# Reordering the end of an attention and soft-MoE kernel: last attention tiles, filler matmuls, weight pieces and output groups

## The chip, the cores and the metric

The kernel runs on one core of one Trainium2 chip. The time is device microseconds for one execution, from the program's start to its end. Inputs and outputs lie in HBM in float32; the matrix work is done in bf16 with float32 sums. PE is the matrix engine, ACT and DVE the two engines that read its results out of PSUM, POOL the engine that issues the loads (they cast to bf16 on the way), SP the one that issues the stores.

## The reference

Pooled attention for 8 batches and 8 heads (576 queries, 64 columns per head; keys and values are averaged over 8 positions to 72), and then a soft mixture of experts on its output:

```
x = softmax(q @ mean8(k).T / 8) @ mean8(v)          # 4608 x 512
logits = x @ phi                                    # 4608 x 32 slots
slot_input = softmax(logits, over the rows).T @ x   # 32 x 512
h = relu(slot_input[e] @ w1[e]); slot_out[e] = h @ w2[e]   # 8 experts, 4 slots each, 512 -> 1024 -> 512
out = softmax(logits, over the slots) @ slot_out    # 4608 x 512
```

`w1` and `w2` are 16.8 MB each in float32, q, k and v 9.4 MB each, the output 9.4 MB.

## The kernel before, in words

**Attention.** The batches go in four pairs, each in two halves of the heads (`qd`). Per step, `score_unit` makes one unit of scores and its exponential on ACT, and `u_tile` makes one of nine tiles of the attention output: PE writes it to PSUM, DVE takes a reciprocal (line 325) and scales the tile into `xsa` (line 331); with `by_scalar` ACT does the scaling in four pieces (line 329). `u_tile` of half `qd` runs for tiles 0 to 3 in the same half and for tiles 4 to 8 in the next one. Tiles 4 to 8 of the very last half are made after the loop, with DVE and ACT in turn.

**Dispatch.** For each pair the logits (`lg`) are summed over the heads, exponentiated on ACT into `ee`, and used as weights to sum the rows of x into 32 slots: nine matmuls into `G_ps` (line 346). Pairs 0 to 2 do this inside the next pair's loop, with the logits summed on PE. For the last pair (`by_vector`) DVE sums the logits of all nine tiles in one instruction (line 338). `turn` transposes `ee` into `cT`.

**Experts.** `hidden` (64 matmuls, line 521) and `turn_hidden` give `hT`. `second_layer` sums into `so_ps` over all experts, 8 groups of rows of w2 for each (line 542). w2 lands in buffers that the attention gives up: experts 0 to 3 in `big`, 4 and 5 in `qTa`, 6 and 7 in `xsa`. The last rows, listed in `PIECES`, come as left and right halves of the 512 columns, first all left halves, then all right ones (line 492); the rows of expert 7 may only be loaded when the last dispatch has read that part of `xsa`.

**Output.** `begin(half)` scales `so_ps` into `so_a` and, with the very last row group of w2 carried separately through `z_ps`/`zT`, makes the first output tiles; `product` multiplies by a tile of `cT` (line 600), `put` scales it by the row's reciprocal sum (`recR`, from `row_sums`) on ACT (line 573) or DVE (line 575). 36 tiles of 128 rows are stored in `GROUPS`; the first tiles are made and stored in halves of the columns, the others whole, one store per group. `busy` issues float32 matmuls into an unused buffer `idle`.

**Order.** Loads are issued by POOL in program order, on one queue; stores by SP in program order. A scheduling layer orders the other engines up to the end of attention; from there on every engine runs in the order written.

Of the kernel before, what the change touches and what calls it, by code (L numbers as in the profile page):

```python
# [18 lines left out]
def kernel(  # L19
# [10 lines left out]
    nc = tc.nc  # L30
# [26 lines left out]
    for rows in (2, 2, 2, 4, 6, 8, 12):  # L57
        GROUPS.append((rows, base))
        base += 128 * rows
# [29 lines left out]
    CUT6 = FJ - 5  # L89
# [13 lines left out]
    UNEVEN = 2560  # L103

    def load_w1(e, n, uneven=False):
        dst = w1_sb[:, e:e + n].rearrange("p e j f -> p e (j f)")
        src = moe_w1[e:e + n].rearrange("e (p j) f -> p e (j f)", j=DJ)
# [85 lines left out]
    nc.vector.memset(hz, 0.0)  # L193
# [12 lines left out]
    def after_k(p):  # L206
        if p + 1 < NP:
            q_sb[p + 1] = load(q, p + 1)
        if p == 1:
            load_w1(0, 1, True)  # L210
# [100 lines left out]
    def u_tile(pair, qd, t, ex, by_scalar=False):  # L311

        ps = ps_u.tile([128, HQ, XW + 1], FP, name="u_ps", tag="u")
# [20 lines left out]
    def dispatch(x, ps, ee, by_vector=False):  # L334

        if by_vector:
            lg = small.tile([128, 9, NS], FP, name="lg", bufs=1)
            nc.vector.reduce_sum(out=lg, in_=x[:, :, :, D:XW].rearrange("p t h c -> p t c h"), axis=AX.X)  # L338
        else:
            lg = ps_m.tile([128, 9, NS], FP, name="lg_ps", tag="m")  # L340
            for h in range(H):
                nc.tensor.matmul(out=lg, lhsT=ident, rhs=x[:, :, h, D:XW], start=(h == 0), stop=(h == H - 1))
        nc.scalar.activation(out=ee, in_=lg.rearrange("p t s -> p t () s").to_broadcast([128, 9, NG, NS]), func=AF.Exp)  # L343
        yield
        for t in range(9):
# [25 lines left out]
    def combine(pair):  # L371
# [3 lines left out]
        parts = dispatch(xs[pair], ps, ee)  # L375
        next(parts)
        yield
        next(parts, None)
# [8 lines left out]
    for g, (rows, base) in enumerate(GROUPS):  # L387
        cols = cT[:, :, base // 2:base // 2 + 64 * rows].rearrange("p r (i s) -> p s r i", s=rows // 2)
        n0 = sum(r for r, _ in GROUPS[:g])
# [3 lines left out]
    if GROUPS[0][0] == GROUPS[1][0] == 2:  # L393
        rest = rest[2:]
        quads.append((0, cT[:, :, 0:256].rearrange("p r (g i) -> p g r i", g=2)))
# [3 lines left out]
    for c, (n, t) in enumerate(quads + rest):  # L399
        for i in range(2 * t.shape[1]):  # L400
            place[n + i] = (i, c)

    def row_sums():
# [6 lines left out]
        sums = consts.tile([NC, 4, 128], FP)  # L410
        nc.scalar.copy(out=sums, in_=ps)
        ps = ps_m.tile([128, 4, NC], FP, name="RT_ps", tag="m")
# [25 lines left out]
    for pair in range(NP):  # L438
        for qd in range(2):
# [5 lines left out]
            for i in range(9):  # L445
# [5 lines left out]
                else:  # L451
                    u_tile(pair, qd, i - 5, ex)
# [96 lines left out]
    turn_hidden(1)  # L549
    nc.vector.reduce_sum(out=recC, in_=C, axis=AX.X)  # L550
# [8 lines left out]
    z_ps = ps_f.tile([128, 2, 128], FP, name="z_ps", tag="f")  # L559
    nc.tensor.matmul(out=z_ps, lhsT=hz, rhs=cT[:, :, 0:128], start=True, stop=True)  # L560
    zT = post.tile([128, 2, 128], BF)
# [6 lines left out]
    def busy(n):  # L568
        nc.tensor.matmul(out=idle[:, 0:n], lhsT=cTf[:, 0:128], rhs=cTf[:, 0:n], start=True, stop=True)

# [8 lines left out]

    out_a = exf.rearrange("p (n c) -> p n c", c=DM)  # L580
# [112 lines left out]
```

## Time and profile before

| | |
|---|---|
| time, median of 3 runs | 176.11 us (175.51 to 181.43) |
| span of the profiled execution | 179.6 us |
| PE, DVE, ACT busy | 129.9, 97.1, 88.3 us |
| loads' queue: share of the span of the 16 DMA engines | 83.9%, 30.48 MB |
| stores' queue (and one load) | 15.0%, 10.49 MB |
| read from and written to HBM | 61.93 MB, 9.44 MB |

The page gives no other time for the profiled execution than its span. A span lies inside its execution's time, so a span of 179.6 us doesn't fit the runs at 175.51 and 176.11 us; among the three it fits only 181.43 us, which would leave 1.9 us around the span. Times of the trace are counted from the span's start.

### The profile page before, as it was taken

How to read it: one execution, taken by the hardware profiler on the slowest of the kernel's cores; microseconds unless marked ns; L12 is line 12 of the kernel's file. 1: busy time of each engine (PE TensorE's matmuls, PEld its weight loads, DVE VectorE, ACT ScalarE, POOL GpSimd, SP SyncE). 2: the span in 40 equal slices, each digit the busy share in tenths (PEclk: the TensorE clock that was granted, in tenths of full speed). 3: DMA queues.
4: the chain of work that ended last, by engine and by line, in shares of the span. 5: the costliest groups of instructions: out<-in, count | busy, mean ns of one | idle time of the engine just before them, and what ended most of it. 6: DMA issues, size and time to landing. Idle time of an engine off the chain costs nothing.

```text
span 179.6 us, 2853 instructions
## 1 busy us (share of the span) xinstructions
PE 129.9 (72%) x1106; PEld 70.2 (39%) x1106; DVE 97.1 (54%) x258; ACT 88.3 (49%) x168; POOL 19.9 (11%) x37
## 2 busy tenths in 40 slices
PE   0006888999899999999998996512996988798000
PEld 0002463565555655556555543300443232333000
DVE  5403353387868588785888629764335000599200
ACT  3201238986887649876599726232012012799100
POOL 7000111052100040000100004000700300000000
PEclk9999999999999999999999669655559999999755
DMA  5999999999999999999999999999999990699995
GB/s 197 242 209 233 207 220 216 213 224 203 204 220 216 216 207 220 225 204 219 208 230 204 221 217 210 228 206 223 214 210 207 196 181 7 225 342 428 480 394 235
DMA packets 10780, 41.13 MB, mean 229 GB/s; under 512 B 768, under 2 KB 6656, under 8 KB 7184
## 3 DMA queue, kind: packets, MB, share of 16 engines
q0 software_dynamic: 7440, 30.48, 83.9%
q1 hardware_dynamic: 3328, 10.49, 15.0%
q8 instruction: 8, 0.13, 0.3%
q14 instruction: 4, 0.03, 0.0%
HBM read 61.93 MB, written 9.44 MB: 397 GB/s over the span
## 4 chain that ended last, share of the span: by engine, by line
PE 51%; ACT 17%; DVE 14%; DMA 6%; issue 3%; POOL 1%; DVEq 0%; ACTq 0%; POOLq 0%
PE pool_ps L234 9%; ACT exa L308 7%; DMA phi_f<-in_moe_phi_dram 6%; PE G_ps L346 6%; PE sc L306 6%; PE u_ps L320 6%; PE q_ps L266 5%; DVE w_sb L575 4%; PE h_ps L521 3%; DVE xsa L331 3%; PE so_ps L542 3%; ACT vmeans L240 2%; DVE lg L338 2%; PE R_ps L407 2%; PE turn_ps L250 2%
## 5 line engine op out<-in xcount | busy, mean ns | idle before, releaser
L308 ACT ACTIVATE exa<-sc 72x576 bf16<-72x576 f32 x64 | 39.5, 652 | 5.1 <-PE sc L306 4.3
L331 DVE TENSOR_TENSOR xsa<-u_ps,rec 128x384 bf16<-128x384 f32 x69 | 37.4, 554 | 1.3
L320 PE MATMUL u_ps<-vp,exa 72*128 72x97 bf16 (+1 forms) x320 | 27.3, 217 | 4.5 <-DVE xsa L331 3.7
L320 PEld LDWEIGHTS <-exa 72*128 72x128 bf16 (+1 forms) x320 | 18.2, 104 | 16.0 <-DVE xsa L331 6.8
L306 PE MATMUL sc<-qTa,kp 64*72 64x288 bf16 x128 | 22.0, 309 | 1.9 <-ACT exa L308 1.5
L234 PE MATMUL pool_ps<-big,pmat 128*128 128x512 bf16 x64 | 18.6, 411 | 0.7 <-ACT qTa L270 0.6
L325 DVE RECIPROCAL rec<-u_ps 128x4 f32<-128x4 f32 x72 | 11.5, 172 | 12.8 <-PE u_ps L320 12.6
L346 PE MATMUL G_ps<-xsa,ee 128*128 128x512 bf16 x36 | 12.0, 496 | 6.6 <-ACT ee L343 6.6
L266 PE MATMUL q_ps<-ident,big 128*128 128x128 bf16 x144 | 12.5, 231 | 0.2
L186 PE MATMUL phi_ps<-spread,sel 128*128 128x256 bf16 x4 | 1.3, 397 | 15.1 <-DVE spread L181 15.1
L600 PE MATMUL f_ps<-so,cT 128*128 128x512 bf16 (+1 forms) x42 | 10.2, 337 | 1.8 <-ACT w_sb L573 0.8
L306 PEld LDWEIGHTS <-kp 64*72 64x72 bf16 x128 | 8.0, 108 | 8.3 <-issue 3.1
L575 DVE TENSOR_SCALAR w_sb<-f_ps,recR 128x512 f32<-128x512 f32 (+1 forms) x17 | 10.5, 683 | 0.4 <-PE f_ps L600 0.2
L266 PEld LDWEIGHTS <-big 128*128 128x128 bf16 x144 | 9.6, 104 | 2.4 <-issue 0.7
L242 DVE TENSOR_REDUCE rsum<-rest_ps 128x64 f32<-128x512 f32 x8 | 5.5, 692 | 9.3 <-PE rest_ps L238 9.2
L270 ACT COPY qTa<-q_ps 128x768 bf16<-128x768 bf16 x8 | 6.3, 794 | 7.8 <-PE q_ps L266 7.8
L272 DVE COPY qTa<-q_ps 128x768 bf16<-128x768 bf16 x16 | 8.8, 553 | 2.1 <-PE q_ps L266 2.0
L573 ACT ACTIVATE w_sb<-f_ps,recR 128x512 f32<-128x512 f32 (+1 forms) x17 | 9.6, 638 | 0.5 <-PE f_ps L600 0.3
L492 POOL DMA_DIRECT2D xsa<-in_moe_w_dram x8 | 6.0, 754 | 26.2 <-PE G_ps L346 15.3
L346 PEld LDWEIGHTS <-ee 128*128 128x128 bf16 x36 | 4.1, 120 | 12.3 <-ACT ee L343 6.8
L234 PEld LDWEIGHTS <-pmat 128*128 128x128 bf16 x64 | 5.8, 103 | 6.4 <-issue 2.3
L240 ACT CAST vmeans<-pool_ps 128x1024 bf16<-128x1024 f32 x4 | 4.0, 1012 | 6.8 <-PE pool_ps L234 6.8
(104 smaller groups left out, 155.1 us busy)
## 6 DMA issues: line engine op xcount, KB each, us to landing
w_sb<-in_moe_w_dram POOLq DMA_DIRECT2D x2, 3072.0 KB, 37.2
big<-in_q_dram POOLq DMA_DIRECT2D x4, 1152.0 KB, 12.0
big<-in_v_dram POOLq DMA_DIRECT2D x4, 1152.0 KB, 15.8
big<-in_moe_w_dram POOLq DMA_DIRECT2D x1, 4096.0 KB, 40.0
big<-in_k_dram POOLq DMA_DIRECT2D x3, 1152.0 KB, 21.4
out_dram<-w_sb SPq DMA_DIRECT2D x1, 3072.0 KB, 10.8
qTa<-in_moe_w_dram POOLq DMA_DIRECT2D x1, 2048.0 KB, 30.4
out_dram<-w_sb SPq DMA_DIRECT2D x1, 2048.0 KB, 7.5
```

What stands on the lines that cost most here:

```text
L234: nc.tensor.matmul(out=ps, lhsT=pmat, rhs=src[:, t:full * POOL:POOL, :], start=(t == 0), stop=(t == POOL - 1))
L266: nc.tensor.transpose(out=ps[:, t].rearrange("p n i -> p (n i)"), in_=q_sb[pair][:, tt:tt + 2, :].rearrange("p t d -> p (t d)"), identity= ...
L272: nc.vector.tensor_copy(out=dst, in_=ps)
L306: nc.tensor.matmul(out=ps[:, r, 0:S // 2], lhsT=kp[pair][rows, n], rhs=qT[pair][rows, n].rearrange("p t i -> p (t i)"), start=True, stop=True)
L308: nc.scalar.activation(out=dst.rearrange("p r (i t) -> p r i t", t=NU), in_=ps[:, :, 0:S // 2].rearrange("p r (t i) -> p r i t", i=NI), fu ...
L320: nc.tensor.matmul(out=ps[rows, hh], lhsT=ex[b][:, hh].rearrange("p r t -> p (r t)")[:, c:c + rows.stop - rows.start], rhs=vp[(2 * pair + ...
L325: nc.vector.reciprocal(out=rec, in_=ps[:, :, XW])
L331: nc.vector.tensor_tensor(out=dst, in0=ps[:, :, 0:XW], in1=rec.rearrange("p h -> p h ()").to_broadcast([128, HQ, XW]), op=ALU.mult)
L346: nc.tensor.matmul(out=ps, lhsT=ee[:, t].rearrange("p g s -> p (g s)"), rhs=x[:, t, :, 0:D], start=(t == 0), stop=(t == 8))
L573: nc.scalar.activation(out=dst, in_=src, func=AF.Copy, scale=by)
L575: nc.vector.tensor_scalar(out=dst, in0=src, scalar1=by, scalar2=None, op0=ALU.mult)
L600: nc.tensor.matmul(out=ps, lhsT=tokens(n), rhs=so[:, cols], start=True, stop=True)
```

## The change

- Of the nine tiles of the last half, ACT scales tiles 1, 3, 5 and 7 (before: 4, 6 and 8); tiles 6, 7 and 8 are written to the score buffers (`spare`), which are free by then.
- The last pair's logits are summed on PE in three parts (`weigh`: tiles 0 to 3, 4 to 6, 7 and 8), each with its own exponential, and summed into `G_ps` part by part (`gather`).
- `row_sums` is split; its ten matmuls stand ahead of `z_ps` now, and its transposes (`turn_sums`) ahead of the second layer.
- The two pairs of 512-column float32 fillers give way to 24 and 40 bf16 fillers of 128 columns (`tiny`); six of 256 columns stand between the right halves.
- Five row groups of expert 6 are loaded whole instead of three, so 11 row groups come in halves instead of 13.
- Four tiles instead of two carry the last row group (`CARRY`), eight tiles instead of ten are made by halves, and groups are 2, 2, 2, 2, 4, 10, 14 rows instead of 2, 2, 2, 4, 6, 8, 12. The right halves are made two and two.
- The first expert's w1 is loaded in one transfer instead of four of unequal shape; one clearing of `hz` goes from DVE to POOL.

```diff
-    for rows in (2, 2, 2, 4, 6, 8, 12):
+    for rows in (2, 2, 2, 2, 4, 10, 14):
...
-    CUT6 = FJ - 5
+    CUT6 = 5
...
-    def load_w1(e, n, uneven=False):
...
-        if uneven:
-            for p0, p1 in ((0, 112), (112, 120), (120, 128)):
-                nc.gpsimd.dma_start(out=dst[p0:p1, :, 0:UNEVEN], in_=src[p0:p1, :, 0:UNEVEN])
-            dst, src = dst[:, :, UNEVEN:], src[:, :, UNEVEN:]
-        nc.gpsimd.dma_start(out=dst, in_=src)
+    def load_w1(e, n):
+        nc.gpsimd.dma_start(out=w1_sb[:, e:e + n].rearrange("p e j f -> p e (j f)"),
+                            in_=moe_w1[e:e + n].rearrange("e (p j) f -> p e (j f)", j=DJ))
...
+    def weigh(x, ee, t0, t1):
+        lg = ps_m.tile([128, t1 - t0, NS], FP, name="lg_ps", tag="m")
+        for h in range(H):
+            nc.tensor.matmul(out=lg, lhsT=ident, rhs=x[:, t0:t1, h, D:XW], start=(h == 0), stop=(h == H - 1))
+        nc.scalar.activation(out=ee[:, t0:t1], in_=lg.rearrange("p t s -> p t () s").to_broadcast([128, t1 - t0, NG, NS]),
+                             func=AF.Exp)
+    def gather(x, ps, ee, t0, t1):
+        for t in range(t0, t1):
             nc.tensor.matmul(out=ps, lhsT=ee[:, t].rearrange("p g s -> p (g s)"), rhs=x[:, t, :, 0:D],
...
-                    u_tile(pair, qd, i - 5, ex)
+                    u_tile(pair, qd, i - 5, ex, by_scalar=pair == NP - 1 and qd == 1 and i in (6, 8))
...
-    u_tile(*last[:2], 4, last[2], by_scalar=True)
-    for i in range(1, 5):
-        u_tile(*last[:2], 4 + i, last[2], by_scalar=i % 2 == 0)
-    for _ in dispatch(xs[NP - 1], G_ps, ee, True):
-        pass
+    for i in range(5):
+        u_tile(*last[:2], 4 + i, last[2], by_scalar=i % 2 == 1, ps=spare[i - 2] if i >= 2 else None)
+        if i == 2:
+            weigh(x, ee, 0, 4)
+    gather(x, G_ps, ee, 0, 4)
+    weigh(x, ee, 4, 7)
+    gather(x, G_ps, ee, 4, 7)
+    weigh(x, ee, 7, 9)
+    gather(x, G_ps, ee, 7, 9)
...
+    row_sums()
     nc.vector.reduce_sum(out=recC, in_=C, axis=AX.X)
...
+    SPLIT, CARRY = 8, 4
...
+    def tiny(count, n=128):
+        for _ in range(count):
+            nc.tensor.matmul(out=idle[:, 0:n], lhsT=cT[:, 0, 0:128], rhs=cT[:, 0, 0:n], start=True, stop=True)
...
+    turn_sums()
+    tiny(24)
     for e in range(4):
         second_layer(e)
-    row_sums()
-    busy(512)
+    tiny(40)
     for e in range(4, E - 2):
         second_layer(e)
-    busy(512)
     second_layer(E - 2, 0, CUT6)
...
     begin(0)
-    tiles(2, 3, 0)
-    tiles(3, 4, 0)
+    tiles(4, 6, 0)
+    second(PIECES[:1], 1)
+    tiles(6, 8, 0)
+    tiny(3, 256)
+    second(PIECES[1:2], 1)
+    tiny(3, 256)
+    second(PIECES[2:-1], 1)
+    begin(1)
     for n in (4, 6):
-        tiles(n, n + 2, 0)
...
+        tiles(n, n + 2, 1)
+    for n in range(SPLIT, len(TILES)):
```

ACT at the end of attention: the last exponentials of the scores, then the tiles that ACT scales (four instructions for one tile) and the exponentials of the logits. Before:

```order
L366 ACTIVATE cT,C<-c_ps 128x2x288
L308 ACTIVATE exa<-sc 72x576
L329 ACTIVATE xsa<-u_ps,rec 128x96 x12
L343 ACTIVATE ee<-lg 128x1152
L526 ACTIVATE h_sb_1719<-h_ps 128x512
```

With the change:

```order
L360 ACTIVATE cT,C<-c_ps 128x2x288
L302 ACTIVATE exa<-sc 72x576
L324 ACTIVATE xsa<-u_ps,rec 128x96 x8
L334 ACTIVATE ee<-lg_ps 128x512
L324 ACTIVATE xsa<-u_ps,rec 128x96 x4
L324 ACTIVATE xsa<-sc,rec 128x96 x4
L334 ACTIVATE ee<-lg_ps 128x384
L334 ACTIVATE ee<-lg_ps 128x256
L533 ACTIVATE h_sb_1749<-h_ps 128x512
```

ACT scales four tiles instead of three, and the first exponential of the logits stands between the second and the third of them; one exponential became three.

SP, the stores of the output (of `exa`: the first groups; `256x1x256` is a pair of half tiles, `128x2048` a group of four whole rows). Before:

```order
L591 DMA out_dram<-exa 128x256 x4
L591 DMA out_dram<-exa 256x1x256
L591 DMA out_dram<-w_sb 128x2x256 x2
L591 DMA out_dram<-exa 128x256 x2
L591 DMA out_dram<-exa 256x1x256 x2
L591 DMA out_dram<-w_sb 512x1x256
L591 DMA out_dram<-w_sb 128x3072
L591 DMA out_dram<-w_sb 128x4096
L591 DMA out_dram<-w_sb 128x6144
```

With the change:

```order
L606 DMA out_dram<-exa 128x256 x2
L606 DMA out_dram<-exa 256x1x256 x3
L606 DMA out_dram<-exa 128x256 x2
L606 DMA out_dram<-exa 256x1x256 x3
L606 DMA out_dram<-w_sb 128x2048
L606 DMA out_dram<-w_sb 128x5120
L606 DMA out_dram<-w_sb 128x7168
```

There are ten stores of half tiles instead of twelve, and the last three carry 4, 10 and 14 rows instead of 6, 8 and 12.

More of the change, by code (lines that the diff above doesn't have):

```diff
@@ L192 @@
     hz = consts.tile([128, 128], BF)
-    nc.vector.memset(hz, 0.0)
+    for i in range(4):
+        nc.gpsimd.memset(hz[:, 32 * i:32 * i + 32], 0.0)
     att = ExitStack()
@@ L386 @@
     quads, rest = [], []
-    for g, (rows, base) in enumerate(GROUPS):
+    g = n0 = 0
+    while g < len(GROUPS):
+        rows, base = GROUPS[g]
+        if rows == 2 and g + 1 < len(GROUPS) and GROUPS[g + 1][0] == 2:
+            quads.append((n0, cT[:, :, base // 2:base // 2 + 256].rearrange("p r (g i) -> p g r i", g=2)))
+            g, n0 = g + 2, n0 + 4
+            continue
         cols = cT[:, :, base // 2:base // 2 + 64 * rows].rearrange("p r (i s) -> p s r i", s=rows // 2)
-        n0 = sum(r for r, _ in GROUPS[:g])
         for r in range(0, rows, 4):
@@ L401 @@
             place[n + i] = (i, c)
+    sums = consts.tile([NC, 4, 128], FP)
     def row_sums():
@@ L558 @@
                             scalar2=None, op0=ALU.mult)
-    z_ps = ps_f.tile([128, 2, 128], FP, name="z_ps", tag="f")
-    nc.tensor.matmul(out=z_ps, lhsT=hz, rhs=cT[:, :, 0:128], start=True, stop=True)
-    zT = post.tile([128, 2, 128], BF)
+    SPLIT, CARRY = 8, 4
+    z_ps = ps_f.tile([128, CARRY, 128], FP, name="z_ps", tag="f")
+    for r in range(0, CARRY, 2):
+        nc.tensor.matmul(out=z_ps[:, r:r + 2], lhsT=hz, rhs=cT[:, :, 64 * r:64 * r + 128], start=True, stop=True)
+    zT = post.tile([128, CARRY, 128], BF)
     nc.scalar.copy(out=zT, in_=z_ps)
@@ L578 @@
     so = post.tile([128, DM], BF)
+    IN_A = 8
     out_a = exf.rearrange("p (n c) -> p n c", c=DM)
```

67 lines of the change are left out of this document (25 added, 42 removed).

## The prediction, made before the changed kernel was run

> **What bounds the kernel now.** I read the timeline of slices first, then the stretches, then the chain that ended last.
>
> ```profile
> DMA  5999999999999999999999999999999990699995
> GB/s 197 242 209 233 207 220 216 213 224 203 204 220 216 216 207 220 225 204 219 208 230 204 221 217 210 228 206 223 214 210 207 196 181 7 225 342 428 480 394 235
> ```
>
> The DMA engines are full from the first slice to 148 us, at some 215 GB/s into SBUF (half of what is read, since the loads cast). Then one slice is nearly empty, and after it the stores fill them again. Loads and stores hardly overlap: two transfers in a row, and between them a hole in which the core computes. The stretches give its edges and the rates (busy time by engine, granted clock, DMA share, GB/s):
>
> ```profile
> 146.00:147.00 1.00, 1.00 (x10) 0.20 (x12) 0.13 (x2) 0.00 (x0) 0.00 (x0) 1.00 1.45 195
> 148.00:149.00 1.00, 1.00 (x5) 0.10 (x3) 0.00 (x0) 0.00 (x0) 0.00 (x0) 1.00 0.33 44
> 152.00:153.00 1.00, 0.68 (x6) 0.46 (x6) 0.48 (x1) 0.85 (x2) 0.00 (x0) 1.00 0.00 0
> 153.00:154.00 1.00, 0.86 (x13) 0.46 (x12) 0.96 (x3) 0.86 (x3) 0.00 (x0) 1.00 0.60 199
> 159.00:160.00 1.00, 1.00 (x5) 0.37 (x4) 1.00 (x2) 1.00 (x3) 0.00 (x0) 1.00 1.03 338
> 162.00:177.90 15.90, 3.93 (x14) 1.40 (x12) 5.41 (x9) 4.47 (x8) 0.00 (x0) 0.69 0.98 416
> 177.00:178.00 1.00, 0.00 (x0) 0.00 (x0) 0.00 (x0) 0.00 (x0) 0.00 (x0) 0.50 0.12 49
> ```
>
> Half rows go out at 338 GB/s, whole rows at 416. The last packet is at 177.9, the end at 179.57, so 1.65 us follow it. Twenty half tiles (131 KB) and 26 whole ones (262 KB) need 7.8 + 16.4 = 24.2 us; from 153.3 that is 177.5, so after the hole the stores alone set the end, with 0.4 us lost. What sets their start is in the chain that ended last (start, length):
>
> ```profile
> 118.22 1.04 ACT xsa L329 x4
> 119.29 4.00 DVE lg L338
> 123.31 1.17 ACT ee L343
> 124.53 4.03 PE G_ps L346 x9
> 128.59 0.69 DVE Gb L353
> 130.33 5.32 PE h_ps L521 x58
> 140.65 3.99 PE R_ps L407 x10
> 144.66 0.58 ACT sums L411
> 145.29 0.41 PE RT_ps L414 x4
> 145.70 1.05 PE idle_ps L569 x2
> 147.73 1.06 PE idle_ps L569 x2
> 151.07 0.48 ACT so_a L573
> ...
> 155.03 0.46 ACT so_a L573
> ```
>
> It runs on compute from 109 to `so_a` at 151.07: serial logits, dispatch, experts, row sums and fillers. No weight of layer two is waited for. Those landed earlier:
>
> ```profile
> xsa<-in_moe_w_dram POOLq DMA_DIRECT2D x1, 192.0 KB, 18.0
> 139.36 0.76 POOL L492 DMA_DIRECT2D xsa<-in_moe_w_dram  x1 [8.97 <-ACT zT L562]
> xsa<-in_moe_w_dram POOLq DMA_DIRECT2D x1, 192.0 KB, 9.7
> ```
>
> The first is the last piece but one of the left half, issued second of the four that begin at 125.86 (0.77 each): 126.6 + 18.0 = 144.7. The other is its partner on the right: 139.36 + 9.7 = 149.1. So there are two bounds close together: compute (151.07) and, behind it, the loads (gates at 144.7 and 149.1).
>
> **The change, part by part.** *Dispatch.* The serial piece from the last tile to the end of `G_ps` (128.56) is broken up. ACT has, from its last score exponential at 110.6, four tiles at 1.04 and three exponentials; 1.17 us for 1152 columns makes these 0.6, 0.5 and 0.35 with a little for starting each. Without any wait that is 5.6 us, to 116.2, and two matmuls of `G_ps` (4.03/9 = 0.45 each) end it at 117.1. Waits come in, because PE takes its instructions in order: logits (8), `G_ps` (2), tile 7, `G_ps` (2), logits (8), `G_ps` (3), logits (8), `G_ps` (2). Of the following rows the first is that last exponential, the second the nearest one for the logits (half clock, 288 columns: 0.28 each; by width about 0.1 here), the others serve the fillers:
>
> ```profile
> 109.95 0.65 ACT L308 ACTIVATE exa<-sc 72x576 bf16<-72x576 f32 x1
> ...
> 100.27 1.14 PE L342 MATMUL lg_ps<-xsa,ident 128*128 128x288 bf16 x4
> 128.34 0.80 PE L361 MATMUL c_ps<-ident,ee 128*128 128x128 bf16 x5
> 40.04 0.84 PE L266 MATMUL q_ps<-ident,big 128*128 128x128 bf16 x12
> ```
>
> Tile 3 leaves ACT at 114.7, its logits and `ee` are done at 115.7, two of `G_ps` at 116.6, tile 7 is scaled at 118.2; then `ee` 119.4, `G_ps` 120.7, logits 121.5, `ee` 121.9, `G_ps` 122.7. I take −5.9 us; the bounds are −11.4 (no wait) and −2.6 (0.4 us more at each of eight hand-offs).
>
> *Fillers.* 64 of 128 columns: by the twelve transposes at full clock 0.07 each, 4.5 us; by the five at half clock 0.16 each, 10.2 us. Gone are 1.05 + 1.06. A second `z_ps` matmul adds 0.3. I take full clock, since the clock had been back for 5 us where they stand (below): +2.7; upper bound +8.4.
>
> *Row sums ahead of `z_ps`.* The same 3.99 us, but the wait for `sums` (144.66 to 145.29) now lies beside `z_ps`: −0.6.
>
> So `so_a` is ready at 151.07 − 5.9 + 2.7 − 0.6 = 147.3. The left gate moves to 145.3, since two more row groups of 64 KB lie ahead of it at 195 GB/s; it is passed with the piece's own matmuls by 145.9. Compute still decides in this execution, by 1.4 us.
>
> *Stores.* `so_a` to first packets was 2.2 us; 149.5 now, and the first half's 1.05 MB last until 152.6. The right `so_a` came 3.96 us after the left one (151.07, 155.03); with eight tiles instead of ten and six fillers between I take 3.6: 150.9, past its gate. Its packets start at 153.1: a hole of 0.5. Halves end at 156.2 (16 × 131 KB: 6.2 us in all). Whole tiles come at this pace:
>
> ```profile
> L575 DVE TENSOR_SCALAR w_sb<-f_ps,recR 128x512 f32<-128x512 f32 x13 | 8.7, 746 | 0.1
> 157.76 9.65 DVE L575 TENSOR_SCALAR w_sb<-f_ps,recR 128x256 f32<-128x256 f32 x15
> ```
>
> 13 in 8.7 us on each of two engines, 0.67 for two. They start some 3.2 us after `so_a` (3.7 before: two half tiles of 0.48 go ahead in the second row, so 158.7 less 155.03), at 154.1. The group of 4 is on its way by 156.3 and done at 158.8. The group of 10 is complete after 7 × 0.67 at 158.8, its packets start 0.9 later: a hole of 0.9. It takes 6.3 us, to 166.0; the group of 14 is ready at 163.5 and takes 8.8, to 174.8; with 1.65 the span is 176.5. **In the frame of the profiled execution the change takes 3.1 us of 179.6.** Before, the smaller groups (6, 8, 12) kept the engines fed without such a hole.
>
> *Edits at nothing.* The single load of w1 moves the same bytes on a queue that is never empty before 148; three POOL issues of 0.5 us fall away and four clearings come there, beside waits of many microseconds. If the uneven shape had evened out the DMA engines, it could show at the end of the loads: they fade out over about 1 us (the row from 148 to 149), so ±0.4.
>
> **How that stands to the runs.** A difference under about 2% is what a measurement of this kernel can't tell from no change. The median is 176.11, and the profiled execution, by its span, is one like 181.43. In the other runs 5.3 us are missing, and the profile shows where such a difference can lie:
>
> ```profile
> 99.66:106.49 6.83, 6.61 (x27) 2.89 (x27) 2.13 (x7) 3.67 (x6) 0.00 (x0) 0.50 1.01 212
> 113.31:120.14 6.83, 2.62 (x28) 1.66 (x25) 3.91 (x11) 3.10 (x12) 0.00 (x0) 0.50 1.02 215
> 126.97:133.79 6.82, 6.64 (x54) 3.00 (x56) 2.95 (x7) 0.00 (x0) 2.65 (x4) 0.50 1.01 211
> 133.79:140.62 6.83, 5.28 (x86) 2.83 (x79) 2.64 (x6) 1.57 (x3) 0.76 (x1) 1.00 1.08 200
> ```
>
> The clock is at half from 99.66 to 106.49 and from 113.31 to 133.79. Without that the chain is some 5 us shorter, `so_a` comes near 146, and the loads are the bound: by my account 149.0 + 24.2 + 1.65 = 174.9, and 174.2 is what 176.11 less 1.9 leaves. **A run near the median already has its stores at the heels of its loads**, and a shorter chain has nothing left to shorten there. With the change such a run has gates at 145.9 and about 149.6 (right `so_a`), whole tiles from 152.8, the group of 10 at 158.4 where the engines are free at 157.6, and its end at 175.2; the same account for before, with 6 rows ready in time, gives 174.7. So +0.5: **176.6 us**, no change that can be told.
>
> The Trainium skill (DMA: Bandwidth & Descriptors, "Issuing engines are not separate DMA queues") says that transfers issued by different engines run on the same 16 DMA engines. By it, stores that start before the loads end only take turns with them, which speaks against any gain from a still earlier start; if they were free, 1 us of overlap would make it 175.6. No store ran beside the loads of the last pieces here, so the trace doesn't show it.
>
> **Rivals.**
> - *Compute binds the ordinary runs too.* For it: 42 us of the chain are compute. Then the 3.1 us show in full, 173.0 us, and with the lower end for the dispatch (5.5 us more, until the left gate stops it after 1.4) 171.6. Against it: the account of loads and stores leaves no room under 174. Chance 0.18, half of it beyond 2%.
> - *Fillers at half clock.* If PE's idle spells leave the clock at half past 137 us, the 64 fillers cost 5.7 us more, all on the chain, ahead of the second layer. `so_a` comes at 153.0, later than before, and everything behind it: span 182.2, time 184. It decides as slower than the median by over 2% from 3 us on, about 34 fillers at half clock. Against it: full clock from 133.79 on. Chance 0.15.
> - *The dispatch isn't shorter.* PE's order makes tile 7 wait for two matmuls of `G_ps`; at −2.6 us the chain is even with the old one, and in ordinary runs only the hole ahead of the group of 10 grows: 177.4. Chance 0.12.
>
> The Trainium skill (TensorE: Matmul & The Clock Gate, "Why this matters for your kernels") holds that at least 4 us of steady work bring the full clock and that idle gaps over about 3 us lose it. The trace agrees in direction, not in size: work from 124.5 on got the clock back at 133.79. By the page the chain without its idle spell would keep full clock, and the profiled frame would come to the 175.2 of the undisturbed one.
>
> **How the numbers follow.** Forecast (no change to be told) 0.55, rivals 0.18, 0.15, 0.12. Faster by over 2% (under 172.6): 0.09. Slower (over 179.6): 0.15. Within: 0.76. The range goes from the first rival's 173.0 to just under the second's bound: 173.0 to 179.6.
>
> **What would show it.** Right: `G_ps` ends 5 to 7 us earlier against the last score exponential; no DVE sum of 4 us; the hole in the DMA row near 149 shrinks to under 2 us; a short dip ahead of the group of 10; the end follows the last packet by 1.6 us. Wrong: fillers of 0.1 us and more, a first store after 152, or loads that end before 147.

## The result, and the profile after

The changed kernel takes 177.43 us (median of 7 runs, 176.53 to 178.33), the kernel before 175.94 in the same comparison (7 runs). The ratio is 1.0089, with a 95% interval of 1.0071 to 1.0108: slower by 0.9%, or 1.57 us (0.0089 × 175.94), which lies within the 2% of the forecast. About three in ten of the runs of the kernel before take 178 to 182 us, and its trace in the prediction is of one of these; the ratios leave them out, and experiment 1 gives the trace that the changed kernel is to be compared with.

The profiled execution took 177.8 us, with a span of 176.0. The timeline of slices of the changed kernel (granted clock, DMA share, GB/s; a slice is 4.4 us):

```profile
PEclk9999999999999999999999998559996996999955
DMA  5999999999999999999999999999999999799994
GB/s 201 224 222 216 214 220 212 224 214 218 207 221 216 219 213 212 220 212 216 216 218 216 218 218 210 220 218 218 210 218 216 200 195 174 240 357 432 432 417 209
```

The empty slice near 150 us is gone; the stores follow the loads directly. One slice at 7 tenths is left (150 to 154 us). The stretches show what it consists of (busy time by engine, granted clock, DMA share, GB/s):

```profile
147.50:149.20 1.70, 1.70 (x10) 0.83 (x9) 0.69 (x3) 1.33 (x3) 0.00 (x0) 0.50 0.85 198
149.20:149.80 0.60, 0.60 (x8) 0.25 (x5) 0.32 (x1) 0.47 (x1) 0.00 (x0) 0.82 0.19 67
149.80:152.00 2.20, 1.84 (x17) 0.92 (x14) 0.33 (x1) 0.95 (x2) 0.00 (x0) 1.00 1.02 345
152.00:154.40 2.40, 2.19 (x13) 1.11 (x11) 1.96 (x5) 2.19 (x6) 0.00 (x0) 1.00 0.38 126
154.40:159.00 4.60, 4.40 (x16) 1.86 (x15) 4.60 (x8) 4.60 (x10) 0.00 (x0) 1.00 1.05 392
159.00:160.00 1.00, 0.80 (x4) 0.36 (x3) 1.00 (x3) 1.00 (x3) 0.00 (x0) 1.00 0.78 328
149.20:174.30 25.10, 11.64 (x55) 5.06 (x52) 11.38 (x19) 11.37 (x21) 0.00 (x0) 0.84 0.91 366
174.30:175.30 1.00, 0.00 (x0) 0.00 (x0) 0.00 (x0) 0.00 (x0) 0.00 (x0) 0.50 0.00 0
```

The loads end at 149.2 and the last store packet at 174.3; 1.7 us follow it. In the 25.1 us between, the engines stand still for 9%, that is 2.3 us: 0.5 at 149.2, 1.5 between 152.0 and 154.4, and 0.2 ahead of the group of 10 rows. The chain that ended last now goes through a transfer (start, length):

```profile
112.85 0.60 ACT ee L334
113.50 1.05 PE G_ps L340 x2
115.84 29.15 DMA xsa<-in_moe_w_dram
145.03 0.31 PE so_ps L549 x3
145.37 0.48 ACT so_a L587
149.92 0.43 PE idle_ps L583 x3
150.62 0.48 ACT so_a L587
```

Between dispatch and second layer no compute stands in it any more. The left gate is at 115.84 + 29.15 = 145.0, and `so_a` follows at 145.37. PE waits for landings ahead of it (of PE's waits between 135 and 152 us; total, times, longest):

```profile
PE so_ps L549 <- DMA xsa<-in_moe_w_dram: 2.0, 3, 1.0
```

### The profile page after: what moved, and what is told of

Its sections match the earlier page's. It is cut to its first block, busy times and chain, and to the rows that moved or that the text cites. A ratio compares the mean times of both kernels' runs of the same rounds, so it can differ in the third digit from the quotient of the medians.

```text
span 176.0 us, 3032 instructions
## 1 busy us (share of the span) xinstructions
PE 131.8 (75%) x1197; PEld 74.7 (42%) x1197; DVE 92.4 (52%) x254; ACT 89.1 (51%) x173; POOL 18.3 (10%) x38
## 4 chain that ended last, share of the span: by engine, by line
PE 39%; DMA 23%; ACT 17%; DVE 8%; issue 3%; POOL 1%; DVEq 0%; ACTq 0%; POOLq 0%
DMA xsa<-in_moe_w_dram 17%; PE pool_ps L228 9%; ACT exa L302 8%; DMA phi_f<-in_moe_phi_dram 7%; PE sc L300 6%; PE u_ps L315 5%; PE q_ps L260 5%; PE G_ps L340 4%; DVE w_sb L589 4%; ACT vmeans L234 2%; PE lg_ps L333 2%; PE f_ps L615 2%; PE turn_ps L244 2%; ACT cT L360 1%; ACT vp L292 1%
## 5 line engine op out<-in xcount | busy, mean ns | idle before, releaser
L326 DVE TENSOR_TENSOR xsa<-u_ps,rec 128x384 bf16<-128x384 f32 x66 | 35.8, 553 | 1.2
L315 PE MATMUL u_ps<-vp,exa 72*128 72x97 bf16 (+1 forms) x304 | 25.8, 214 | 2.0 <-DVE xsa L326 1.2
L300 PE MATMUL sc<-qTa,kp 64*72 64x288 bf16 x128 | 21.4, 302 | 1.8 <-ACT exa L302 1.3
L260 PE MATMUL q_ps<-ident,big 128*128 128x128 bf16 x144 | 11.6, 219 | 0.8 <-DVE qTa L266 0.3
L589 DVE TENSOR_SCALAR exa<-f_ps,recR 128x256 f32<-128x256 f32 x6 | 2.8, 483 | 17.2 <-PE f_ps L613 15.8
L340 PE MATMUL G_ps<-xsa,ee 128*128 128x512 bf16 x36 | 10.5, 427 | 1.8 <-ACT ee L334 1.7
L260 PEld LDWEIGHTS <-big 128*128 128x128 bf16 x144 | 8.7, 97 | 2.9 <-issue 1.3
L589 DVE TENSOR_SCALAR w_sb<-f_ps,recR 128x512 f32<-128x512 f32 x14 | 9.3, 744 | 0.1
L587 ACT ACTIVATE w_sb<-f_ps,recR 128x512 f32<-128x512 f32 x14 | 8.4, 694 | 0.2
L587 ACT ACTIVATE so_a<-so_ps,recC 128x256 bf16<-128x256 f32 x2 | 0.9, 474 | 13.7 <-PE so_ps L549 13.7
```

Of the source, the lines that this page charges most:

```text
L260: nc.tensor.transpose(out=ps[:, t].rearrange("p n i -> p (n i)"), in_=q_sb[pair][:, tt:tt + 2, :].rearrange("p t d -> p (t d)"), identity= ...
L300: nc.tensor.matmul(out=ps[:, r, 0:S // 2], lhsT=kp[pair][rows, n], rhs=qT[pair][rows, n].rearrange("p t i -> p (t i)"), start=True, stop=True)
L315: nc.tensor.matmul(out=ps[rows, hh], lhsT=ex[b][:, hh].rearrange("p r t -> p (r t)")[:, c:c + rows.stop - rows.start], rhs=vp[(2 * pair + ...
L326: nc.vector.tensor_tensor(out=dst, in0=ps[:, :, 0:XW], in1=rec.rearrange("p h -> p h ()").to_broadcast([128, HQ, XW]), op=ALU.mult)
L340: nc.tensor.matmul(out=ps, lhsT=ee[:, t].rearrange("p g s -> p (g s)"), rhs=x[:, t, :, 0:D], start=(t == 0), stop=(t == 8))
L587: nc.scalar.activation(out=dst, in_=src, func=AF.Copy, scale=by)
```

## The experiments

All ratios are to the kernel before, in runs on the same chip. Experiments 1 to 4, 5 to 8 and 9 to 12 ran on three different chips, so they are compared by their ratios and not by their times. Each trace is one execution, and its time can lie about 1 us from the median of its kernel; the table at the end of this section gives both.

**1. The kernel before, unchanged.** No edit.

> The kernel before, unchanged, for a trace of one of its runs near the median (175.9 us; the trace shown so far is of one that takes 181.4). Theory A (holes among the stores): the last load lands at 149.4 as in the other trace, the first store's packets start by 149, and from there to the last packet the DMA engines are empty for less than 1.5 us in all, against some 2.9 us with the change (149, 152.0 to 154.3, 159.2). Rival B (PE's clock): no such difference in holes; instead the clock is at full between 145 and 150, where it is at half with the change. Rival C (shape of the first w1 load): the last load lands by 149.0 or earlier, 0.5 us or more ahead of the changed kernel's 149.5. Ratio to itself 1.000, within 0.003.

Measured: 176.06 us, ratio 0.9993 (0.9978 to 1.0008). The profiled execution took 175.5, span 173.6. Its timeline of slices (4.3 us each), then its stretches at the end, then the last matmuls on PE ahead of the left `so_a`:

```profile
PEclk9999999999999999999999998555699999999655
DMA  5999999999999999999999999999999999999994
```

```profile
147.30:148.60 1.30, 1.16 (x14) 0.37 (x12) 1.07 (x4) 1.09 (x3) 0.00 (x0) 1.00 1.11 266
149.30:149.85 0.55, 0.29 (x2) 0.09 (x1) 0.00 (x0) 0.21 (x1) 0.00 (x0) 1.00 0.40 136
149.85:155.00 5.15, 4.55 (x21) 2.07 (x22) 4.36 (x9) 4.84 (x11) 0.00 (x0) 1.00 1.03 343
148.60:172.00 23.40, 10.28 (x43) 4.25 (x42) 11.25 (x19) 11.20 (x21) 0.00 (x0) 0.79 0.99 393
107.40:124.50 17.10, 7.97 (x48) 4.11 (x49) 8.76 (x18) 4.27 (x13) 2.75 (x4) 0.50 1.03 216
```

```profile
144.66 0.40 PE L542 MATMUL so_ps<-xsa,hT 128*32 128x256 bf16 x7
144.99 0.28 PE L597 MATMUL f_ps<-xsa,zT 128*128 128x256 bf16 x1
```

This is the ordinary execution that the prediction inferred without seeing it. The clock is at half from 107.4 to 124.5, across the dispatch, and not again until 162.0, when PE's work is done; the last matmuls of the left half run from 144.66 without idle time ahead of them (it would stand in brackets), and `so_a` starts at 145.11. The first stores go out beside the last loads (266 GB/s). From the loads' end at 148.6 to the last packet 23.4 us pass, with 1% of holes. So the compute chain of the kernel before arrives just when its weights do, and the changed kernel's loss stands in two terms: the loads end 0.6 later (149.2), and the stretch behind them is 1.7 us longer (25.1), which with 0.1 at the end makes the 2.4 between the two spans. These two executions lie further apart (175.5 and 177.8) than the medians do, so their holes overstate the 1.57 us. All three signs named beforehand are there together, fewer holes, a full clock between 145 and 150 and an earlier end of the loads, so this trace doesn't choose between the theories.

**2. Without the six fillers between the right halves.**

```diff
-    tiny(3, 256)
...
-    tiny(3, 256)
```

> The changed kernel without the six fillers of 256 columns between the right halves. Theory A: they are 0.9 us of the 5.25 us between the left and the right scaling of so_ps (145.37, 150.62), during which the first half's stores (3.1 us) run dry; without them the right scaling comes up to 0.9 us earlier (its weights have landed by 149.1), the hole at 152 shrinks, and the time falls by 0.5 to 0.9 us, to 176.5 to 176.9 (ratio 1.003 to 1.006). Rival B: the fillers hold the clock; without them the output's matmuls run at half clock and the time is the same or longer, 177.4 to 178.2.

Measured: 176.65 us, ratio 1.0071 (1.0039 to 1.0102). The stretch behind the loads' end, and the one in which the changed kernel has its clock at half:

```profile
149.10:173.00 23.90, 10.57 (x44) 4.53 (x43) 11.06 (x18) 10.92 (x20) 0.00 (x0) 0.78 0.95 384
146.00:149.40 3.40, 2.49 (x22) 1.03 (x20) 1.84 (x4) 2.26 (x6) 0.00 (x0) 1.00 1.08 209
```

In its trace the right `so_a` starts at 149.37 instead of 150.62 and the stretch is 1.2 us shorter; but the clock is at full here from 146.0 to 149.4, so the trace doesn't separate the fillers from the clock. The runs confirm little of that: 0.0018 or 0.3 us, inside both intervals. The fillers are not the main cause.

**3. Groups of 4, 6, 8 and 10 rows instead of 4, 10, 14.**

```diff
-    for rows in (2, 2, 2, 2, 4, 10, 14):
+    for rows in (2, 2, 2, 2, 4, 6, 8, 10):
```

> The changed kernel with the whole rows in groups of 4, 6, 8, 10 instead of 4, 10, 14. Theory A: the hole ahead of the group of 10 (0.4 to 0.5 us at 159.2) closes, since a group of 6 is complete two tiles' time earlier; everything else stays: 0.4 to 0.6 us less, 176.9 (ratio 1.005). If the larger groups are worth something by themselves (fewer, longer packets) it is 177.4 or more, because the page shows 8 KB to 28 KB packets all near 430 GB/s I expect nothing of that.

Measured: 176.43 us, ratio 1.0043 (1.0026 to 1.0060), an interval that doesn't meet the changed kernel's. So undoing the sizes of the groups gains about 0.0046 × 175.94 = 0.8 us. The trace has no dip where the group of 10 had its own (second row); the third row is ahead of the groups:

```profile
149.10:172.90 23.80, 10.74 (x46) 4.28 (x44) 11.06 (x18) 10.91 (x20) 0.00 (x0) 0.84 0.96 386
158.50:160.00 1.50, 1.17 (x4) 0.47 (x4) 1.50 (x3) 1.40 (x4) 0.00 (x0) 1.00 1.17 492
146.00:149.40 3.40, 3.19 (x28) 1.65 (x27) 1.84 (x4) 2.23 (x5) 0.00 (x0) 1.00 0.98 189
```

This execution differs from the changed kernel's in more than its groups. The output stage runs at full clock, the right `so_a` comes at 149.58 instead of 150.62, and the hole between 152.0 and 154.4 is smaller too (DMA share 0.72 instead of 0.38), where the sizes of the later groups play no part. How much of the 0.8 us is the dip, the trace doesn't tell.

**4. Ten tiles by halves and the groups of before**, with the four carried tiles and the right fillers kept.

```diff
-    for rows in (2, 2, 2, 2, 4, 10, 14):
+    for rows in (2, 2, 2, 4, 6, 8, 12):
...
-    SPLIT, CARRY = 8, 4
+    SPLIT, CARRY = 10, 4
```

> The changed kernel with the old tail: groups 2, 2, 2, 4, 6, 8, 12 and ten tiles by halves (the four carried tiles and the fillers stay). Theory A: 1.3 instead of 1.05 MB of the left half go out while the right half is made, so the hole at 152 is 0.75 us shorter, and the hole at 159 is gone; two more tiles by halves cost 0.3 us of slower packets: 176.5 (ratio 1.003). Rival B: no change, 177.4, since the clock at half sets when the halves come. Rival C: no change.

Measured: 176.36 us, ratio 1.0029 (0.9999 to 1.0060); 23.8 us from the loads' end to the last packet in its trace. About 1.05 us of the 1.57 come back (0.0060 × 175.94), no more than 0.25 beyond what the groups gave by themselves, which the intervals don't tell apart. The stretch in which the changed kernel has its largest hole:

```profile
152.00:154.40 2.40, 2.11 (x13) 1.10 (x11) 1.89 (x6) 2.30 (x6) 0.00 (x0) 1.00 0.66 222
```

In this trace the clock is at half from 142.2 to 149.0 and the right `so_a` comes at 150.51, much as in the changed kernel (146.0 to 149.4, and 150.62). So, unlike those of experiments 2 and 3, the two traces can be compared at like clocks: the share is 0.66 instead of 0.38, 0.7 us less of holes in this stretch. Two more tiles by halves fill part of the wait for the right half, as far as one trace of each can show it.

**5. The kernel before with the shorter dispatch alone** (`weigh` and `gather` in three parts, the four tiles on ACT).

```diff
-    for _ in dispatch(xs[NP - 1], G_ps, ee, True):
-        pass
...
+            weigh(x, ee, 0, 4)
+    gather(x, G_ps, ee, 0, 4)
+    weigh(x, ee, 4, 7)
+    gather(x, G_ps, ee, 4, 7)
+    weigh(x, ee, 7, 9)
+    gather(x, G_ps, ee, 7, 9)
```

> The kernel before with one part of the change alone: the last attention tiles (ACT scaling 1, 3, 5, 7, spare score buffers) and the dispatch in three parts; fillers, weights' pieces and the output's order as before. Theory A: in the run whose trace was shown, compute was late, but in ordinary runs the loads set the start of the stores, so a chain that is about 6 us shorter gains nothing there: ratio 0.997 to 1.000, 175.4 to 175.9. Rival D (compute binds ordinary runs as well): 1.5 to 3 us less, ratio 0.983 to 0.992. If slow runs (181) come from a late chain, none of them should appear here.

Measured: 178.0 us, ratio 1.0086 (1.0054 to 1.0117). The dispatch is shorter by nearly as much as in the changed kernel (last score exponential to the end of `G_ps` 13.2 us, against 18.0 in experiment 1), and the kernel is slower, by as much as with the whole change. The same 4.6 us just behind the loads' end, first of this kernel and then of the kernel before in experiment 1:

```profile
149.40:154.00 4.60, 4.22 (x18) 1.90 (x16) 2.32 (x6) 3.50 (x9) 0.00 (x0) 0.50 0.78 263
149.00:174.40 25.40, 11.66 (x43) 4.72 (x42) 11.37 (x19) 11.40 (x21) 0.00 (x0) 0.70 0.90 359
```

```profile
149.40:154.00 4.60, 3.89 (x20) 1.83 (x20) 3.36 (x7) 3.95 (x10) 0.00 (x0) 1.00 0.96 320
```

The left `so_a` starts at the same time in both (145.00 and 145.11): the gate stops the shorter chain, and PE waits 0.7 us for a landing there. In this execution the chain leads by little more than that, since the clock was at half from 99.4 to 106.2 too and the last score exponential ends 3.6 us later than in experiment 1 (110.06 and 106.46). Behind the gate the output stage runs at half clock here, PE needs 4.22 us for 18 matmuls instead of 3.89 for 20, and the stores lack rows for 22% of the time.

**6. The changed kernel with 30 more fillers in the waits for landings** (14, 5 and 11 of 128 columns).

```diff
+    tiny(14)
...
+        tiny((0, 5, 11)[i])
```

> The changed kernel with 30 more fillers of 128 columns where PE waits for landings ahead of the left half (14, 5 and 11, about 2 us, as long as the waits of 1.0, 0.3 and 0.7 us and a little over). Rival B: PE's idle spells there cost it the full clock from 146.0 to 149.4; with the waits filled the clock stays at full, the left half's tiles come faster and the time falls to the quick end of the changed kernel's runs, 176.5 (ratio 1.003), with little spread. Theory A: the holes are made by the order and the size of the halves; the clock moves the time by 0.3 us at most: 177.1 to 177.7.

Measured: 177.41 us, ratio 1.0070 (1.0045 to 1.0095); only its times are used. In five of its runs the mean clock of the execution was 0.932 to 0.934, and these took 177.02 to 177.49 us. Three runs of experiment 7, nearly the changed kernel and on the same chip, had 0.933 to 0.935 and took 176.47 to 176.81. So with a mean clock as high as the changed kernel's best the filled waits gained nothing; in which stages the clock was full no trace shows. Whether the fillers themselves, which stand ahead of the landed pieces in PE's order, took the gain, this run doesn't tell.

**7. The changed kernel with the uneven load of the first w1.**

```diff
+            for p0, p1 in ((0, 112), (112, 120), (120, 128)):
+                nc.gpsimd.dma_start(out=dst[p0:p1, :, 0:UNEVEN], in_=src[p0:p1, :, 0:UNEVEN])
...
-            load_w1(0, 1)
+            load_w1(0, 1, True)
```

> The changed kernel with the first w1 load in the old four uneven transfers. Rival C: the uneven split evens out the DMA engines at the end of the loads; the last load lands 0.4 us or more earlier and the time falls by as much, 177.0 or less (ratio 1.006 or less). Theory A: no difference, 177.4, ratio 1.009 within 0.002.

Measured: 177.18 us, ratio 1.0047 (1.0018 to 1.0075), which meets the changed kernel's interval at its edge: inconclusive. The traces show no mechanism. The loads end at 149.1 (149.2 in the changed kernel), and the stretch behind them is 25.1 us with either shape.

**8. The changed kernel without its 64 fillers.**

```diff
-    tiny(24)
...
-    tiny(40)
```

> The changed kernel without the 64 fillers of 128 columns ahead of the second layer. Theory A: the left half waits for its weights' landing (145.0) whether or not PE fills the time, so the chain keeps its end; only the clock suffers: PE idles some 4 us more ahead of 139, and may run at half clock until the loads' end: 177.4 to 178.4. If the fillers delay the chain (as in the rival of the prediction) the time falls below 177.

Measured: 178.11 us, ratio 1.0110 (1.0081 to 1.0139). Without the fillers the kernel isn't faster, so they don't delay it; whether they help is not shown, since the interval meets the changed kernel's. Its trace shows the second layer at half clock, and the longest stretch of all behind the loads:

```profile
137.30:144.10 6.80, 6.68 (x56) 2.50 (x58) 0.40 (x2) 1.13 (x2) 1.33 (x2) 0.50 1.25 198
148.40:175.40 27.00, 12.40 (x62) 5.50 (x60) 12.19 (x21) 12.50 (x24) 0.00 (x0) 0.80 0.88 350
```

The left `so_a` starts at 146.64, 1.3 us later than with the fillers. But this execution was late before the fillers' place: its clock was at half from 99.8 to 106.6 too, and the last score exponential ends at 110.67, 3.6 us later than in the changed kernel's trace. So the trace doesn't give a price for the second layer at half clock.

**9. The changed kernel with the whole tail of before** (13 row groups by halves, two carried tiles, ten tiles by halves, groups 2, 2, 2, 4, 6, 8, 12, no right fillers); dispatch, row sums, 64 fillers and w1 as changed.

```diff
-    for rows in (2, 2, 2, 2, 4, 10, 14):
+    for rows in (2, 2, 2, 4, 6, 8, 12):
...
-    CUT6 = 5
+    CUT6 = FJ - 5
...
-    SPLIT, CARRY = 8, 4
+    SPLIT, CARRY = 10, 2
```

> The changed kernel up to the left half (shorter dispatch, row sums ahead, 64 small fillers, even w1), and from there the tail of before: groups 2, 2, 2, 4, 6, 8, 12, ten tiles by halves, two carried tiles, three whole row groups of expert 6, no fillers between the right halves. Theory A (the tail's order and sizes make the holes): the loss goes, ratio 1.000 to 1.003. Theory B (a chain that arrives early lets PE idle and lose its clock, and then everything after it is late): most of the loss stays, ratio 1.006 to 1.009, as with the short chain alone (1.0086).

Measured: 176.4 us, ratio 1.0025 (0.9997 to 1.0052). The tail holds 0.0064 × 175.94 = 1.1 us of the loss; the rest, 0.4, can't be told from nothing. Yet experiment 5 has this tail and this dispatch too and takes 1.0086, and the two intervals just don't meet. What differs between them is the place of the row sums, the fillers, the shape of w1 and the clearing of `hz`. So the loss is not a sum of one part for the tail and one for the dispatch.

**10. Three edits undone at once**: groups 4, 6, 8, 10; no right fillers; uneven w1.

```diff
-    for rows in (2, 2, 2, 2, 4, 10, 14):
+    for rows in (2, 2, 2, 2, 4, 6, 8, 10):
...
-            load_w1(0, 1)
+            load_w1(0, 1, True)
...
-    tiny(3, 256)
...
-    tiny(3, 256)
```

> The changed kernel with three edits taken back together: whole rows in groups of 4, 6, 8, 10, no fillers between the right halves, the uneven first w1 load. Alone they took 0.5%, 0.2% and 0.4% off 1.0089. If they add up, as holes in one row of stores do (theory A), the ratio is 0.998 to 1.001, 175.7 to 176.1. If they are the same gain seen three times (the chip's luck with the clock, theory B), it stays at 1.004 or more.

Measured: 176.54 us, ratio 1.0051 (1.0026 to 1.0076). The single gains of 2, 3 and 7 (0.0018, 0.0046, 0.0042) don't add up to 0.0106; all three together are worth no more than the groups alone. Its trace has the clock at half from 147.3 to 154.1, and 24.6 us behind the loads' end.

**11. The kernel before without its float32 fillers**, four pairs of matmuls.

```diff
-    busy(512)
...
-        if n:
-            busy(n)
```

> The kernel before without its four float32 fillers: the same chain, 3.4 us shorter, and nothing to keep PE busy until the weights land. Theory B: PE waits for landings ahead of the left half, the clock falls to half in the output stage, and the stores show holes: slower by 0.7 to 1.5%, ratio 1.007 to 1.015, and no run of 180 or more, since the late chain behind those is now shorter. Theory A: the start of the stores is set by the loads and the order behind it is unchanged: ratio 0.998 to 1.001.

Measured: 177.21 us, ratio 1.0055 (1.0022 to 1.0087). Less work makes the chain shorter too, and again the kernel is slower. PE's wait for landings between 135 and 152 us, and the stretches:

```profile
PE so_ps L542 <- DMA xsa<-in_moe_w_dram: 3.3, 4, 1.3
```

```profile
140.80:144.20 3.40, 0.86 (x12) 0.21 (x9) 0.00 (x0) 0.00 (x0) 0.59 (x1) 1.00 1.45 195
144.20:154.40 10.20, 9.09 (x43) 3.77 (x43) 4.55 (x10) 6.36 (x15) 0.00 (x0) 0.50 0.98 227
149.00:173.80 24.80, 12.13 (x45) 4.88 (x44) 11.38 (x19) 11.39 (x21) 0.00 (x0) 0.71 0.93 368
```

PE is idle for 2.5 of the 3.4 us before 144.2, and then the clock is at half for 10.2 us, over the whole stage in which the stores start. Its runs lie in two groups: five of 175.92 to 176.11 us at a mean clock of 0.898 to 0.910, seven of 177.17 to 177.64 at 0.890 to 0.893.

**12. Experiment 5 with 48 bf16 fillers of 128 columns ahead of the second layer.**

```diff
+    for _ in range(48):
+        nc.tensor.matmul(out=idle[:, 0:128], lhsT=cT[:, 0, 0:128], rhs=cT[:, 0, 0:128], start=True, stop=True)
```

> The kernel before with the shorter dispatch (as in the run of that part alone, 1.0086) and 48 fillers of 128 columns ahead of the second layer, about 2.9 us at full clock, which give most of the gain of the chain away again. Theory B: PE no longer waits at the landings, the clock holds, and the time comes back to before's: ratio 0.998 to 1.002. If the shorter dispatch costs by itself (its stores or its loads in another place), the ratio stays at 1.007 or more.

Measured: 177.78 us, ratio 1.0104 (1.0052 to 1.0156). A ratio near 1, which fillers that keep the clock would have given, did not come; it is the 1.007 or more that was named for a dispatch that costs by itself. But the fillers didn't keep the clock, so the run doesn't decide between the two. It rests on four runs, of 176.73 to 178.37 us, and the trace is of the fastest of them:

```profile
146.00:149.40 3.40, 3.29 (x21) 1.50 (x20) 1.82 (x4) 2.28 (x5) 0.00 (x0) 0.50 1.16 196
149.30:173.20 23.90, 10.46 (x44) 4.24 (x44) 11.28 (x19) 11.20 (x21) 0.00 (x0) 0.79 0.97 386
```

The clock is at half from 146.0 to 149.4, just as in the changed kernel, and yet only 23.9 us follow the loads' end in this trace. Half clock in that place alone doesn't set the holes. Why its other runs took up to 1.6 us longer, no trace shows.

**Together.** From the traces, one execution each: the loads' end, the length from there to the last packet, the part of it that the DMA share leaves open, and the time of the execution.

| kernel | loads end | to the last packet | share | of it open, us | time of this execution | ratio of the runs |
|---|---|---|---|---|---|---|
| before (1) | 148.6 | 23.4 | 0.99 | 0.2 | 175.5 | 0.9993 |
| changed | 149.2 | 25.1 | 0.91 | 2.3 | 177.8 | 1.0089 |
| 2, no right fillers | 149.1 | 23.9 | 0.95 | 1.2 | 176.56 | 1.0071 |
| 3, smaller groups | 149.1 | 23.8 | 0.96 | 1.0 | 176.4 | 1.0043 |
| 4, ten halves | 149.5 | 23.8 | 0.97 | 0.7 | 176.78 | 1.0029 |
| 9, tail of before | 149.5 | 23.8 | 0.96 | 1.0 | 176.66 | 1.0025 |
| 7, uneven w1 | 149.1 | 25.1 | 0.91 | 2.3 | 177.37 | 1.0047 |
| 10, three undone | 148.8 | 24.6 | 0.94 | 1.5 | 176.53 | 1.0051 |
| 5, dispatch alone | 149.0 | 25.4 | 0.90 | 2.5 | 177.99 | 1.0086 |
| 11, before without fillers | 149.0 | 24.8 | 0.93 | 1.7 | 177.25 | 1.0055 |
| 8, without the 64 fillers | 148.4 | 27.0 | 0.88 | 3.2 | 178.96 | 1.0110 |
| 12, dispatch and fillers | 149.3 | 23.9 | 0.97 | 0.7 | 176.73 | 1.0104 |

No kernel has its loads' end earlier than 148.4 or later than 149.5, whatever its dispatch, fillers or w1. What differs most is how well the stores are fed behind it, and none of the versions is shown to beat the kernel before. Where the trace is of a fast execution of its kernel, as for 12, a short stretch says little about the ratio.

## Why the prediction was right, point by point

The forecast was no change that can be told, 176.6 us; it is 177.43, inside the range and on the side that the sum gave. The bounds were right. That the time came so near owes something to luck, since the sum missed the stage in which most of the holes are and priced the fillers in the wrong place.

**The bounds.** Right, and shown: an ordinary run of the kernel before is bound by loads and stores (experiment 1: 148.6 + 23.4 + 1.6 = 173.6, the whole span). The account had 149.0 + 24.2 + 1.65. The right half waits for its weights there, 0.3 us until 149.00. "A run near the median already has its stores at the heels of its loads" is what this trace shows, and it is why 5 us off the compute chain brought no gain (experiment 5 alone isn't faster either). The first rival, compute binding the ordinary runs too, fell: the left `so_a` starts at 145.11 before the change and at 145.37 after it.

**Dispatch.** Predicted −5.9, measured −5.2. The timeline of the changed kernel, five groups on ACT and PE (start, length, in brackets the idle time ahead):

```profile
106.46 0.65 ACT L302 ACTIVATE exa<-sc 72x576 bf16<-72x576 f32 x1
119.30 0.61 PE L340 MATMUL G_ps<-xsa,ee 128*128 128x512 bf16 x2 [0.48 <-ACT ee L334]
126.46 4.98 PE L405 MATMUL R_ps<-cT,onehot 128*10 128x512 bf16 x10
132.50 2.74 PE L583 MATMUL idle_ps<-cT 128*128 128x128 bf16 x24
137.28 2.41 PE L583 MATMUL idle_ps<-cT 128*128 128x128 bf16 x40
```

From the end of the last score exponential (107.11) to the end of `G_ps` (119.91) are 12.8 us; in experiment 1 they are 18.0. Most of both is at half clock (108.5 to 118.7 here, 107.4 to 124.5 there). The rival that the dispatch isn't shorter (−2.6) fell.

**Fillers.** Predicted 4.5 us for the 64, measured 2.74 + 2.41 = 5.2: 0.06 each for the 40, and 0.11 for the 24, which did run at half clock, from 132.35 to 135.8. As a price on the path the term was wrong in kind: PE still waits 2.0 us for landings behind the fillers, and without them the kernel isn't faster (178.11). The rival of fillers at half clock described a part of the trace and fell in what it would cost.

**Row sums ahead of `z_ps`.** Predicted −0.6 with 3.99 us for `R_ps` as before. `R_ps` took 4.98 us, 1.0 more. It too lies ahead of the gate, and nothing waited for it at the end.

**Stores.** The gates are right: 145.3 predicted and 145.0 measured for the left one, 149.1 predicted for the right one, where the loads end at 149.2. The size of the loss is the step that failed: +0.5 predicted, +1.57 measured. The hole ahead of the group of 10 was to be 0.8 us in an ordinary run (158.4 less 157.6). The trace shows the dip in its place, but 0.2 to 0.4 us of it; the runs of experiment 3 give 0.8 for undoing the groups, and its trace leaves open by which path. What the account took at zero in ordinary runs is the stage around the right halves. It put the right `so_a` at about 149.6, and it came at 150.62, behind a left output stage at half clock:

```profile
146.00:149.40 3.40, 3.40 (x17) 1.66 (x16) 1.74 (x4) 1.95 (x5) 0.00 (x0) 0.50 1.00 177
```

The product of the halves took 342 ns each instead of 272 (the groups by shape, changed kernel and experiment 1):

```profile
L615 PE MATMUL f_ps<-so,cT 128*128 128x256 bf16 x8 | 1.8, 342 | 0.2 <-DVE so L589 0.2
```

```profile
L600 PE MATMUL f_ps<-so,cT 128*128 128x256 bf16 x16 | 2.7, 272 | 1.0 <-DVE so L575 0.6
```

With eight tiles by halves instead of ten there is also less to store until whole tiles come: 2.0 us of holes between 149.2 and 154.4, where the trace of before has 0.3 (149.30 to 149.85). The trace of experiment 4 agrees at a like clock: with ten tiles by halves 0.7 us less of holes from 152.0 to 154.4. With the rest of the change in place the tail of before gives back 1.1 of the 1.57 (experiment 9); that it isn't a separate part of the loss is shown by experiment 5, which has that tail and loses as much.

**The signs named beforehand.** There: no DVE sum of 4 us, no hole of 2 us near 149 (0.5), a dip ahead of the group of 10, 1.7 us behind the last packet, and stores that go out before the loads' end, far from the 152 that would have spoken against it. The fillers of 0.1 us and more came for 24 of 64.

**Edits at nothing.** w1's shape moves the loads' end by 0.1 us. A small effect on the times is neither shown nor excluded (experiment 7).

**The clock.** The prediction counted the half clock of the profiled execution as a disturbance and gave the changed kernel full clock for the ordinary run. That was wrong by the trace of the changed kernel, and one stretch at half clock lies just ahead of the unforeseen part of the loss. The ordinary execution of the kernel before wasn't free of it either (107.4 to 124.5 in experiment 1). The Trainium skill (TensorE: Matmul & The Clock Gate, "What's actually happening") describes a gate that judges PE's activity in windows of about 3.4 us. The trace agrees with that: the stretches at half clock until the end of PE's work are 10.2, 3.45 and 3.4 us long (108.5 to 118.7, 132.35 to 135.8, 146.0 to 149.4). The same page's "Why this matters for your kernels" asks for no idle gap above about 3 us. Here the clock fell at 146.0 though the longest wait ahead was 1.0 us:

```profile
139.20:142.60 3.40, 2.38 (x32) 1.14 (x29) 0.00 (x0) 0.00 (x0) 1.09 (x2) 1.00 1.27 193
142.60:146.00 3.40, 2.11 (x16) 0.97 (x15) 0.00 (x0) 0.47 (x1) 0.17 (x1) 1.00 1.45 197
```

After a stretch of 3.4 us with 2.38 us of work the clock stayed, after one with 2.11 it fell. The busy time isn't the rule, though. In experiment 2 the clock stayed at full (until 162.6) after less work:

```profile
138.70:142.10 3.40, 2.08 (x32) 0.96 (x29) 0.00 (x0) 0.00 (x0) 0.74 (x1) 1.00 1.21 193
```

What decides, these traces don't show.

**What stays open** is why a chain that arrives early costs 1 to 1.8 us (experiments 5, 11 and 12) when the left gate is passed at the same time, and why it costs next to nothing in experiment 9. For the clock: half clock lies across the output stage until about 154 in the traces of 5, 10 and 11, which leave 1.5 to 2.5 us open; the two groups of runs of experiment 11 part by their mean clock; and the changed kernel's runs at a mean clock of 0.933 take 176.5 us, those of 0.924 and less 177.35 to 178.33. Against it as the only cause: experiment 6 had as high a mean clock and not the time, and experiments 9 and 12 had the changed kernel's half clock from 146.0 to 149.4 with 1.0 and 0.7 us open instead of 2.3. The runs allow that the clock is a part, and don't settle it.

## What to carry to other kernels

Look for the trace of an ordinary run before shortening a chain: where the last landing and the last matmul already meet, a shorter chain can move nothing, and here its slack came back as waits at the landings and, in the traces, a clock at half in the stage behind them. When stores follow at the heels of loads, judge every edit of the tail by the first microseconds behind the loads' end: are there rows to send in each of them, and is each group complete before the one ahead has gone out. Fillers that look like dead weight may hold the clock; take them out in a run of their own before counting them as a price.

## What the runs showed of the hardware

- The end of the loads hardly moves with these edits: 148.4 to 149.5 in twelve traces with different dispatch, fillers and w1.
- PE's busy time doesn't tell whether the clock holds. After 2.08 us of 3.40 it held in experiment 2 (138.7 to 142.1, above). The stretch ahead of the fall at 132.35 in the changed kernel is busy for 3.06 of 3.40 us, with 11 matmuls, among them the last of the 10-column sums:

```profile
128.95:132.35 3.40, 3.06 (x11) 0.67 (x9) 0.00 (x0) 0.87 (x2) 0.79 (x1) 1.00 1.05 222
```

- Stores that run beside loads seem to take turns with them. From 147.3 to 148.6 experiment 1 moves 266 GB/s, a rate between that of the last loads alone (195 to 197, the rows of 142.6 to 146.0 and 140.8 to 144.2) and that of stores alone (343, from 149.85). The Trainium skill (DMA: Bandwidth & Descriptors, "Issuing engines are not separate DMA queues") says just this of transfers from different engines, and the trace, which could not show it before, agrees.
